# Score products in 32 x 32 pieces, and a new order for the opening of a two-layer transformer kernel

## Chip, cores and metric

The kernel runs on one core of a Trainium2 chip. The metric is the device time of one execution in microseconds (us). TensorE is called PE here, VectorE DVE, ScalarE ACT, GpSimd POOL, and SyncE SP. PE multiplies a stationary operand, which a weight load brings into its array of 128 rows by 128 columns, with a moving operand, and writes PSUM. The other three compute engines do the rest of the arithmetic. SP and ACT issue the transfers of this kernel.

## What is computed

The input x has 2048 rows of 512 numbers in bfloat16. Two layers are applied, each of an attention with 32 heads of 16 dimensions and a feed-forward part with a hidden width of 1792; both layers use the same weights.

```python
def _A_ref(x, wqkv, wo):
    B, S, D = x.shape
    H = 32; Dh = D // H
    qkv = (lambda x, *d: x.transpose(*d))((x @ wqkv).reshape(B, S, 3, H, Dh), 2, 0, 3, 1, 4)
    q, k, v = qkv[0], qkv[1], qkv[2]
    scale = Dh ** -0.5
    scores = jnp.einsum("bhqd,bhkd->bhqk", q, k) * scale
    p = _softmax(scores, axis=-1)
    o = jnp.einsum("bhqk,bhkd->bhqd", p, v)
    return (lambda x, *d: x.transpose(*d))(o, 0, 2, 1, 3).reshape(B, S, D) @ wo

def _B_ref(x, w1, w2):
    h = _silu(jnp.einsum("bsd,df->bsf", x, w1))
    return jnp.einsum("bsf,fd->bsd", h, w2)

x = A_x
x = x + _A_ref(_layernorm(x, axis=-1), A_wqkv, A_wo)
x = x + _B_ref(_layernorm(x, axis=-1), B_w1, B_w2)
x = x + _A_ref(_layernorm(x, axis=-1), A_wqkv, A_wo)
x = x + _B_ref(_layernorm(x, axis=-1), B_w1, B_w2)
```

## The kernel before

**Tiles.** Attention goes by segments: four heads (a head block, hb) by 512 queries (a chunk, c). Within a segment, a score tile is 128 keys by 512 queries for two of the four heads. Each head has 32 rows of the array: 16 for its dimensions and further ones by which a bound on the scores is subtracted. So a score tile is two products (L1214), each with a stationary operand of 32 rows by 128 columns (`KT`, keys) and a moving operand of 32 rows by 512 (`QT`, queries). Each of the two writes one bank of a slot of PSUM. There are three slots. PE may issue one tile or, when two slots are free, two tiles together; four products with different rows then run side by side.

**From scores to output.** Most slots are read by ACT, which writes the exponential in bfloat16 (L1429). About every fifth is read by DVE, which makes an approximation of the exponential by integer arithmetic (L1459), from which POOL (L1520) or DVE (L1493) derives three shifted copies. The value products (L1290) multiply the rows with the values, 17 columns a head (16 dimensions and a column of ones for the sum), in four column strips of the array, one for each head, and add up in `q_ps`.

**Background work.** Projections, the output product, layer norm and the feed-forward part are pieces that are woven between the score tiles. Their products come from the helper `mm` (L282), which while `whole[0]` is false cuts each in four column strips of 128 rows by 32 columns; in the opening and the ending they are whole (L278). Fillers (L1325) keep PE's clock up where nothing else is ready; beside score products they take 32 rows and 16 columns.

**Order.** Each of the four compute engines executes its instructions in the order in which they are written. In the main part a planner (`Flow`) fixes that order when the program is built: it keeps a clock for each engine with fixed costs (`MM`, `SWITCH` and others) and picks, for each engine in turn, the next step. What it picks does not depend on the measured times. The method `scores` writes a tile's products. The planner's order is the same before and after the change, since no cost of it is changed.

**Opening.** Up to the first score tile a list written out by hand, `OPENING`, gives the order: a word such as `s10` is a step and its numbers. s are statistics of a row tile, sq the square root, r the reciprocal, a the normalisation (L201), t a transpose on PE (L215), c its copy by ACT (L1593), k, h and m the keys of the first head block, v and e the values, q, o, u, b, z and y the first queries, w fillers, x a table load. The first digit is the chunk. Ahead of it stand the set-up steps: the loads, constants on POOL, and the weaving of the raw weights `wraw` into `wkq` by POOL (L144), first for five heads, then for the others. These set-up steps are written outside of the manual order, so that their place on each engine is chosen by the framework's own scheduler; the manual order is entered just ahead of `OPENING`.

Of the kernel before, what the change touches and what calls it, by code (L numbers as in the profile page):

```python
# [12 lines left out]
FP32 = mybir.dt.float32  # L13
BF16 = mybir.dt.bfloat16
# [6 lines left out]
def kernel(  # L21
# [22 lines left out]
    NQC = S // 512  # L44
# [3 lines left out]
    EPS = 1e-5  # L48
    KR = 32
    VW = DH + 1  # L50
# [14 lines left out]
    cpool = ctx.enter_context(tc.tile_pool(name="cpool", bufs=1))  # L65
    wpool = ctx.enter_context(tc.tile_pool(name="wpool", bufs=1))
    xpool = ctx.enter_context(tc.tile_pool(name="xpool", bufs=1))
# [17 lines left out]
        return gpool.tile([P, 512], FP32, name=name, tag="g")  # L85


    x_sb = xpool.tile([P, TT, D], BF16, name="x_sb")
    for tt in range(4):
        (nc.scalar if tt % 2 else nc.sync).dma_start(x_sb[:, tt, :], xf[tt * P : (tt + 1) * P, :])  # L90
    for c in range(1, NQC):
        nc.sync.dma_start(
            x_sb[:, 4 * c : 4 * c + 4, :],
            xf[512 * c : 512 * (c + 1), :].rearrange("(tt p) d -> p tt d", p=P),
        )
    wv_sb = wpool.tile([P, CT, D], BF16, name="wv_sb")
    wo_sb = wpool.tile([P, CT, D], BF16, name="wo_sb")
    w1_sb = wpool.tile([P, CT, F], BF16, name="w1_sb")
    w2_sb = wpool.tile([P, FT, D], BF16, name="w2_sb")


    wkq = wpool.tile([P, CT, 2 * D + DH], BF16, name="wkq")
    wraw = htpool.tile([P, CT, 2 * D], BF16, name="wraw", tag="ht")
    nc.scalar.dma_start(wraw[:], A_wqkv[:, 0 : 2 * D].rearrange("(ct p) f -> p ct f", p=P))
    nc.scalar.dma_start(wv_sb[:], A_wqkv[:, 2 * D : 3 * D].rearrange("(ct p) f -> p ct f", p=P))
    nc.sync.dma_start(wo_sb[:], A_wo.rearrange("(ct p) e -> p ct e", p=P))
    nc.sync.dma_start(w1_sb[:], B_w1.rearrange("(ct p) f -> p ct f", p=P))
    nc.sync.dma_start(w2_sb[:], B_w2.rearrange("(ft p) e -> p ft e", p=P))

    ident = cpool.tile([P, P], BF16, name="ident")  # L110
    make_identity(nc, ident[:])
    eps_t = cpool.tile([P, 1], FP32, name="eps_t")
    nc.vector.memset(eps_t[:], EPS)
# [3 lines left out]
    half = cpool.tile([P, 4, 1], FP32, name="half")  # L117
    nc.gpsimd.memset(half[:], -0.5)
# [6 lines left out]
    nc.gpsimd.memset(wkq[:, :, 2 * D : 2 * D + DH], 0.0)  # L125
    E = cpool.tile([P, P], FP32, name="E")
    nc.gpsimd.memset(E[:], 0.0)
    sel = cpool.tile([P, 2, P], BF16, name="sel")
    for j in range(4):
        one = slice(32 * j + 16, 32 * j + 17)  # L130
        nc.gpsimd.tensor_copy(out=E[:, one], in_=ident[:, one])
        nc.gpsimd.memset(E[32 * j : 32 * j + 16, one], -1.0)
        for i in range(2):
# [5 lines left out]
    for lo, hi in ((0, 5), (5, H)):  # L139
        for t in range(2):  # L140
            for ct in range(CT):
                pairs = wkq[:, ct, 0 : 2 * D].rearrange("p (h t d) -> p h t d", t=2, d=DH)
                raw = wraw[:, ct, (1 - t) * D : (2 - t) * D].rearrange("p (h d) -> p h d", d=DH)
                nc.gpsimd.tensor_copy(out=pairs[:, lo:hi, t, :], in_=raw[:, lo:hi, :])  # L144
# [4 lines left out]
    v_flat, x_flat = (xpool.tile([P, TT * H * VW], BF16, name=f"v{i}") for i in range(2))  # L149
    vs = [  # L150
        v[:].rearrange("p (t h w) -> p t h w", t=TT, h=H) for v in (v_flat, x_flat)
    ]
# [82 lines left out]
    def dve(ns, fn, g=""):  # L235
        return ("dve", ns, fn, g)
# [59 lines left out]
    def bank(cell, name):  # L296
        cell["ps"] = narrow(name)
# [36 lines left out]
    def ones_v(L, lo, hi):  # L334
        nc.gpsimd.memset(vs[L][:, lo:hi, :, DH:VW], 1.0)
# [566 lines left out]
    class Flow:  # L902
# [291 lines left out]
        def scores(self, at, picks):  # L1194

            if self.mode != "R":
                at += SWITCH
            self.mode = "R"
            two = len(picks) == 2
            self.pe = at + (MM + 8 if two else MM + 3)  # L1200
            self.runs.append((at, at + MM))
            new = []
            for k in picks:
                t = Tile(self.n)
                self.n += 1
                if t.seg.i > self.started:
                    self.started = t.seg.i
                    self.begin(t.seg)
                if t.pr == 0 and t.kt != t.seg.kts[0]:
                    self.pace(t.seg, t.kt - t.seg.kts[0])  # L1210
                t.slot, t.at = k, at
                for jj in range(2):
                    j = 2 * t.pr + jj
                    nc.tensor.matmul(  # L1214
                        self.slots[k][:, jj, :],
                        lhsT=KT[32 * j : 32 * j + KR, t.seg.hb, t.kt * P : (t.kt + 1) * P],
                        rhs=t.seg.QT[32 * j : 32 * j + KR, :],
                        start=True,
                        stop=True,
                    )  # L1220
# [331 lines left out]
    HOT = 0.9  # L1552
    MOST = 2600

    ordered = {
        mybir.EngineType.PE, mybir.EngineType.Activation, mybir.EngineType.DVE, mybir.EngineType.Pool
    }
# [57 lines left out]
    def o_e(c, i):  # L1615
        tt = 4 * c + 2 * i
        nc.scalar.copy(
            vs[0][:, tt : tt + 2, :, 0:DH],
            at["v", c, i][:].rearrange("p t (h d) -> p t h d", d=DH),
        )  # L1620
        ones_v(0, tt, tt + 2)
        v_made.update([(0, tt), (0, tt + 1)])

    def o_q(_):
# [33 lines left out]
    for word in OPENING.split():  # L1658
        name, args = word.rstrip("0123456789"), [int(d) for d in word if d.isdigit()]
# [49 lines left out]
```

## Time and profile before

| | |
|---|---|
| median of 3 runs | 1651.63 us (1651.11 to 1653.09) |
| the profiled execution | 1650.25 us, span of its trace 1648.5 us |
| PE | 1568.1 us busy, 17480 products |
| ACT | 1592.4 us busy |
| DVE | 1154.7 us busy |
| POOL | 1213.2 us busy |
| first score product | at 37.42 us |

The trace starts with the first instruction of the program. A row of a timeline gives the start, the length from the first to the last of the merged instructions, the engine, the line, what is written and read, and how many instructions. "PEld" are weight loads. In brackets stands the idle time before the row, with what ended it. PE's ends are modelled: a product of 512 columns is recorded with some 380 ns, though the next on the same part of the array starts after about 0.22 us. The chain is the work that ended last, followed back from the end.

### The profile page before, as it was taken

The page shows a single profiled execution, that of the slowest core. Times are in us where ns is not written, and L with a number is a line of the kernel's source. Part 1 is how long each engine was busy: PE and PEld are TensorE (multiplying, and loading weights), DVE is VectorE, ACT ScalarE, POOL GpSimd, SP SyncE. Part 2 cuts the span into 40 slices and gives each one's busy share as a digit, 9 for nine tenths or more (in the row PEclk, how much of TensorE's full clock was granted, in tenths as well). Part 3 has the DMA queues.
Part 4 walks back from the last instruction along what each step waited for, and adds up shares of the span by engine and source line. Part 5 has one row for each costly group of instructions (what it writes and reads, how often), then busy time and mean ns, then how long its engine had stood idle before and what let it go on. Part 6 is the DMA issues. An engine that isn't in the chain of part 4 may idle for free.

```text
span 1648.5 us, 42491 instructions
## 1 busy us (share of the span) xinstructions
PE 1568.1 (95%) x17480; PEld 506.5 (31%) x17480; DVE 1154.7 (70%) x1463; ACT 1592.4 (97%) x1807; POOL 1213.2 (74%) x1290
## 2 busy tenths in 40 slices
PE   7999999999999999999999998999999999999998
PEld 3222223233333333233333232222223323333333
DVE  6778877766777666657776556887666786686744
ACT  5999999999999999999999998999999999999993
POOL 2888988896787767756666654877767897899850
PEclk9999999999999999999999999999999999999999
DMA  5000001010110001000000000011000000010000
GB/s 192 5 8 8 8 5 20 21 8 5 33 21 5 8 21 30 9 8 17 21 15 2 2 14 8 11 11 30 18 8 14 25 21 8 14 34 11 11 24 13
DMA packets 83682, 30.77 MB, mean 19 GB/s; under 512 B 75552, under 2 KB 82464, under 8 KB 83488
## 3 DMA queue, kind: packets, MB, share of 16 engines
q1 hardware_dynamic: 82000, 26.10, 7.2%
q8 instruction: 136, 2.23, 0.6%
q10 hardware_dynamic: 1488, 1.97, 0.3%
q14 instruction: 58, 0.48, 0.1%
HBM read 7.86 MB, written 2.10 MB: 6 GB/s over the span
## 4 chain that ended last, share of the span: by engine, by line
PE 58%; ACT 22%; DVE 8%; issue 6%; POOL 4%; DMA 2%; ACTq 0%; DVEq 0%; POOLq 0%
PE slot L1214 20%; PE q_ps L1290 17%; ACT p L1429 14%; PE y_ps L282 7%; PE q_ps L282 3%; PE h_ps L282 3%; ACT v L1429 3%; PE k_ps L282 3%; ACT t_sb L546 2%; POOL p L1520 2%; DVE p L1459 2%; DVE hT L550 1%; DMA at<-oT 1%; ACT q_old L1429 1%; PE v_ps L282 1%
## 5 line engine op out<-in xcount | busy, mean ns | idle before, releaser
L1429 ACT ACTIVATE p<-slot 128x1024 bf16<-128x1024 f32 x1186 | 1189.8, 1209 | 11.1 <-PE slot L1214 10.3
L1520 POOL TENSOR_TENSOR p<-p,steps 128x512 int32<-128x512 int32 x569 | 595.3, 1069 | 241.9 <-DVE p L1459 201.8
L1290 PE MATMUL q_ps<-p,v 128*17 128x512 bf16 x4590 | 520.9, 382 | 4.3 <-ACT p L1429 1.1
L1214 PE MATMUL slot<-QT,KT 32*128 32x512 bf16 x3104 | 441.9, 381 | 24.3 <-ACT p L1429 10.4
L1459 DVE TENSOR_SCALAR p<-slot 128x1024 uint16<-128x1024 f32 x282 | 344.3, 1221 | 136.1 <-PE slot L1214 121.1
L1214 PEld LDWEIGHTS <-KT 32*128 32x128 bf16 x4096 | 193.3, 91 | 580.5 <-issue 575.3
L1429 ACT ACTIVATE v<-slot 128x1024 bf16<-128x1024 f32 x295 | 338.9, 1234 | 1.7 <-PE slot L1214 1.6
L1290 PEld LDWEIGHTS <-v 128*17 128x17 bf16 x6574 | 165.6, 88 | 286.2 <-issue 225.4
L1290 PE MATMUL q_ps<-v,v 128*17 128x512 bf16 x1302 | 202.8, 381 | 1.9 <-DVE oT L1118 0.9
L1520 POOL TENSOR_TENSOR p<-v,steps 128x512 int32<-128x512 int32 x123 | 129.5, 1066 | 47.6 <-DVE v L1459 34.9
L1520 POOL TENSOR_TENSOR v<-p,steps 128x512 int32<-128x512 int32 x138 | 146.2, 1067 | 23.9 <-DVE p L1459 23.3
L1429 ACT ACTIVATE q_old<-slot 128x1024 bf16<-128x1024 f32 x130 | 154.1, 1222 | 1.0 <-PE slot L1214 1.0
L282 PE MATMUL h_ps<-xnT,w_sb 128*32 128x512 bf16 x1568 | 130.7, 384 | 9.9 <-DVE hT L550 8.9
L1214 PE MATMUL slot<-q_old,KT 32*128 32x512 bf16 x896 | 124.4, 381 | 7.6 <-ACT p L1429 4.9
L1459 DVE TENSOR_SCALAR v<-slot 128x1024 uint16<-128x1024 f32 x82 | 100.1, 1220 | 37.1 <-PE slot L1214 34.9
L550 DVE SCALAR_TENSOR_TENSOR hT<-t_sb,h_ps 128x512 bf16<-128x512 f32 x98 | 66.9, 683 | 79.4 <-ACT t_sb L546 79.4
L282 PE MATMUL y_ps<-w_sb,hT 128*32 128x512 bf16 x1568 | 119.4, 382 | 1.4 <-DVE qc L359 1.1
L1290 PE MATMUL q_ps<-q_old,v 128*17 128x512 bf16 x572 | 98.3, 381 | 1.5 <-DVE q_old L1493 0.7
L282 PE MATMUL q_ps<-xnT,wkq 128*32 128x512 bf16 x1008 | 82.1, 383 | 2.1 <-DVE hT L550 1.2
L282 PE MATMUL k_ps<-xnT,wkq 128*32 128x512 bf16 x960 | 79.3, 383 | 1.8 <-DVE hT L550 0.7
L546 ACT ACTIVATE t_sb<-h_ps 128x512 f32<-128x512 f32 x98 | 76.4, 780 | 0.1
L1520 POOL TENSOR_TENSOR v<-v,steps 128x512 int32<-128x512 int32 x59 | 62.7, 1069 | 10.9 <-DVE v L1459 10.9
(162 smaller groups left out, 1543.6 us busy)
## 6 DMA issues: line engine op xcount, KB each, us to landing
w_sb<-in_B_w_dram SPq DMA_DIRECT2D x2, 1792.0 KB, 15.2
out_dram<-x_sb SPq DMA_DIRECT2D x15, 128.0 KB, 1.7
x_sb<-in_A_x_dram SPq DMA_DIRECT2D x3, 512.0 KB, 10.3
wraw<-in_A_wqkv_dram ACTq DMA_DIRECT2D x1, 1024.0 KB, 8.7
at<-oT SPq DMA_TRANSPOSE x63, 2.3
xnT<-hT SPq DMA_TRANSPOSE x44, 2.3
wv_sb<-in_A_wqkv_dram ACTq DMA_DIRECT2D x1, 512.0 KB, 10.9
wo_sb<-in_A_wo_dram SPq DMA_DIRECT2D x1, 512.0 KB, 11.2
```

Source lines behind the costliest of these rows:

```text
L282: nc.tensor.matmul(ps[g, :], lhsT=lhsT[:, g], rhs=rhs, start=start, stop=stop, skip_group_check=True)
L546: nc.scalar.activation(t_sb, ps, ACT.Tanh, scale=0.5)
L550: nc.vector.scalar_tensor_tensor(out=hT[:, ft, :], in0=t_sb, scalar=1.0, in1=ps, op0=ALU.add, op1=ALU.mult)
L1214: nc.tensor.matmul(self.slots[k][:, jj, :], lhsT=KT[32 * j : 32 * j + KR, t.seg.hb, t.kt * P : (t.kt + 1) * P], rhs=t.seg.QT[32 * j : 32 * ...
L1290: nc.tensor.matmul(self.o_ps[32 * j : 32 * j + VW, :], lhsT=vs[seg.L][:, t.kt, 4 * seg.hb + j, :], rhs=buf[:, jj, :], start=not seg.opened ...
L1429: nc.scalar.activation(buf[:].rearrange("p a b -> p (a b)"), self.slots[x.slot][:].rearrange("p a b -> p (a b)"), ACT.Exp, scale=float(SCALE),
L1459: nc.vector.tensor_scalar(out=whole.bitcast(U16), in0=self.slots[x.slot][:].rearrange("p a b -> p (a b)"), scalar1=float(UNIT), scalar2=fl ...
L1520: nc.gpsimd.tensor_tensor(out=b1.bitcast(I32), in0=b0.bitcast(I32), in1=steps32[:, k : k + 1].to_broadcast([P, 512]), op=ALU.add,)
```

## The change

Three things are changed.

1. Each score product is split in four of 32 columns: product g reads 32 of the 128 keys and writes 32 of the 128 partitions of the same bank. All have the same moving operand.
2. The manual order is entered ahead of the set-up, so that it too runs in written order. The set-up is rewritten: loads of the first five heads' query and key columns come first, ahead of the values' weights, and the other heads' columns follow the input on SP's queue; POOL writes all ones of the first layer's `v` in one step ahead of the first weave, where before each value step wrote its own.
3. `OPENING` is reordered: among other things k0 stands ahead of v00, and sq1 ahead of e00.

```diff
+    ctx.enter_context(tc.manual_schedule(engines=ordered))
...
-    nc.scalar.dma_start(wraw[:], A_wqkv[:, 0 : 2 * D].rearrange("(ct p) f -> p ct f", p=P))
+    FIRST = 5
+    def load_x(c, queue):
+        queue.dma_start(
+            x_sb[:, 4 * c : 4 * c + 4, :],
+            xf[512 * c : 512 * (c + 1), :].rearrange("(tt p) d -> p tt d", p=P),
+        )
+    def load_kq(lo, hi, queue):
+        for t in range(2):
+            at = slice(D * t + DH * lo, D * t + DH * hi)
+            queue.dma_start(wraw[:, :, at], A_wqkv[:, at].rearrange("(ct p) f -> p ct f", p=P))
+    for tt in range(4):
+        (nc.scalar if tt % 2 else nc.sync).dma_start(x_sb[:, tt, :], xf[tt * P : (tt + 1) * P, :])
+    load_kq(0, FIRST, nc.scalar)
+    load_x(1, nc.sync)
     nc.scalar.dma_start(wv_sb[:], A_wqkv[:, 2 * D : 3 * D].rearrange("(ct p) f -> p ct f", p=P))
+    load_x(2, nc.sync)
+    load_x(3, nc.sync)
+    load_kq(FIRST, H, nc.sync)
...
+    def ones_v(L, lo, hi):
+        nc.gpsimd.memset(vs[L][:, lo:hi, :, DH:VW], 1.0)
...
+    def weave(lo, hi):
+        for t in range(2):
+            for ct in range(CT):
+                pairs = wkq[:, ct, 0 : 2 * D].rearrange("p (h t d) -> p h t d", t=2, d=DH)
+                raw = wraw[:, ct, (1 - t) * D : (2 - t) * D].rearrange("p (h d) -> p h d", d=DH)
+                nc.gpsimd.tensor_copy(out=pairs[:, lo:hi, t, :], in_=raw[:, lo:hi, :])
+
     E = cpool.tile([P, P], FP32, name="E")
...
+    ones_v(0, 0, TT)
+    weave(0, FIRST)
+    sel = cpool.tile([P, 2, P], BF16, name="sel")
...
+    weave(FIRST, H)
...
-            ones_v(L, tt, tt + 1)
+            if L:
+                ones_v(L, tt, tt + 1)
...
-                    nc.tensor.matmul(
-                        self.slots[k][:, jj, :],
-                        lhsT=KT[32 * j : 32 * j + KR, t.seg.hb, t.kt * P : (t.kt + 1) * P],
-                        rhs=t.seg.QT[32 * j : 32 * j + KR, :],
-                        start=True,
-                        stop=True,
-                    )
+                    for g in range(0, P, 32):
+                        nc.tensor.matmul(
+                            self.slots[k][g : g + 32, jj, :],
+                            lhsT=KT[32 * j : 32 * j + KR, t.seg.hb, t.kt * P + g : t.kt * P + g + 32],
+                            rhs=t.seg.QT[32 * j : 32 * j + KR, :],
+                            start=True,
+                            stop=True,
+                            skip_group_check=True,
+                        )
...
-    ctx.enter_context(tc.manual_schedule(engines=ordered))
-
     OPENING = """
-        w9 s00 s01 s02 s03 sq0 r0 a00 a01 t00 a02 t01 c00 a03 t02 s10 c01 t03 c02 s11 v00 c03 s12 s13
-        k0 e00 s20 v01 sq1 h0 r1 a10 a11 a12 t10 a13 e01 t11 s21 q0 c10 s22 t12 c11 t13 s23 c12 v10 c13
-        s30 sq2 r2 a20 a21 e10 t20 a22 t21 a23 k1 s31 c20 c21 t22 s32 t23 h1 v20 s33 c22 c23 m0 sq3 k2
-        r3 e20 a30 a31 t30 a32 t31 c30 a33 t32 o0 c31 t33 c32 v21 u0 c33 m1 h2 x0 m2 k3 v11 e21 h3
-        w2 m3 b0 e11 z0 w3 y0
+        w9 s00 s01 s02 s03 sq0 r0 a00 a01 t00 a02 t01 c00 a03 t02 s10 c01 t03 c02 s11 c03 s12 k0 s13 v00
+        h0 sq1 r1 a10 v01 a11 e00 a12 a13 s20 t10 s21 e01 t11 q0 s22 c10 t12 c11 s23 t13 c12 v10 s30 sq2
+        c13 r2 a20 a21 k1 a22 e10 a23 s31 t20 t21 c20 t22 s32 c21 t23 c22 s33 v20 c23 m0 sq3 h1 r3 a30
+        a31 e20 t30 a32 t31 a33 k2 c30 m1 c31 t32 o0 t33 h2 v21 u0 c32 m2 c33 x0 k3 v11 e21 h3 m3 b0 e11
+        w2 z0 w3 y0
     """
...
-        ones_v(0, tt, tt + 2)
```

More of the change, by code (lines that the diff above doesn't have):

```diff
@@ L85, in narrow @@
         return gpool.tile([P, 512], FP32, name=name, tag="g")
+    ordered = {
+        mybir.EngineType.PE, mybir.EngineType.Activation, mybir.EngineType.DVE, mybir.EngineType.Pool
+    }
+    ctx.enter_context(tc.manual_schedule(engines=ordered))
     x_sb = xpool.tile([P, TT, D], BF16, name="x_sb")
[L89 to L94, printed above, removed]
-        )
     wv_sb = wpool.tile([P, CT, D], BF16, name="wv_sb")
@@ L108 @@
     nc.sync.dma_start(w2_sb[:], B_w2.rearrange("(ft p) e -> p ft e", p=P))
+    v_flat, x_flat = (xpool.tile([P, TT * H * VW], BF16, name=f"v{i}") for i in range(2))
+    vs = [
+        v[:].rearrange("p (t h w) -> p t h w", t=TT, h=H) for v in (v_flat, x_flat)
+    ]
+    def ones_v(L, lo, hi):
+        nc.gpsimd.memset(vs[L][:, lo:hi, :, DH:VW], 1.0)
+    eps_t = cpool.tile([P, 1], FP32, name="eps_t")
+    nc.vector.memset(eps_t[:], EPS)
+    nc.gpsimd.memset(wkq[:, :, 2 * D : 2 * D + DH], 0.0)
     ident = cpool.tile([P, P], BF16, name="ident")
     make_identity(nc, ident[:])
-    eps_t = cpool.tile([P, 1], FP32, name="eps_t")
-    nc.vector.memset(eps_t[:], EPS)
+    half = cpool.tile([P, 4, 1], FP32, name="half")
+    nc.gpsimd.memset(half[:], -0.5)
     steps32 = cpool.tile([P, len(SHIFTS)], I32, name="steps32")
@@ L116 @@
         nc.gpsimd.memset(steps32[:, k : k + 1], SHIFTS[k] * 65537)
-    half = cpool.tile([P, 4, 1], FP32, name="half")
-    nc.gpsimd.memset(half[:], -0.5)
     cols = cpool.tile([P, 2], FP32, name="cols")
@@ L124 @@
     own, onescol = (cols[:, i : i + 1] for i in range(2))
-    nc.gpsimd.memset(wkq[:, :, 2 * D : 2 * D + DH], 0.0)
+    def weave(lo, hi):
[4 more added lines that the diff above has]
+                nc.gpsimd.tensor_copy(out=pairs[:, lo:hi, t, :], in_=raw[:, lo:hi, :])
     E = cpool.tile([P, P], FP32, name="E")
     nc.gpsimd.memset(E[:], 0.0)
-    sel = cpool.tile([P, 2, P], BF16, name="sel")
     for j in range(4):
@@ L132 @@
         nc.gpsimd.memset(E[32 * j : 32 * j + 16, one], -1.0)
-        for i in range(2):
+    ones_v(0, 0, TT)
+    weave(0, FIRST)
+    sel = cpool.tile([P, 2, P], BF16, name="sel")
+    for i in range(2):
+        for j in range(4):
             nc.gpsimd.tensor_copy(
@@ L138 @@
     nc.gpsimd.tensor_scalar_mul(out=sel[:, 1, :], in0=sel[:, 1, :], scalar1=-1.0)
[L139 to L144, printed above, removed]
+    weave(FIRST, H)
     KT = xpool.tile([P, HB, S], BF16, name="KT")
@@ L148 @@
     xnTs = [xpool.tile([P, CT, 512], BF16, name=f"xnT{c}") for c in range(NQC)]
[L149 to L152, printed above, removed]
     o_old = [v_flat[:, 1024 * hb : 1024 * (hb + 1)].bitcast(FP32) for hb in range(HB)]
@@ L332 @@
     v_made = set()
-    def ones_v(L, lo, hi):
-        nc.gpsimd.memset(vs[L][:, lo:hi, :, DH:VW], 1.0)
     def v_piece(tt, L):
```

4 lines of the change are left out of this document (removed).

## The prediction

> **What bounds the kernel now.** I read the page first: busy shares, then the chain that ended last, then the costly groups.
>
> ```profile
> span 1648.5 us, 42491 instructions
> ...
> PE 1568.1 (95%) x17480; PEld 506.5 (31%) x17480; DVE 1154.7 (70%) x1463; ACT 1592.4 (97%) x1807; POOL 1213.2 (74%) x1290
> ...
> PE 58%; ACT 22%; DVE 8%; issue 6%; POOL 4%; DMA 2%; ACTq 0%; DVEq 0%; POOLq 0%
> PE slot L1214 20%; PE q_ps L1290 17%; ACT p L1429 14%; PE y_ps L282 7%; PE q_ps L282 3%; PE h_ps L282 3%; ACT v L1429 3%; PE k_ps L282 3%; ACT t_sb L546 2%; POOL p L1520 2%; DVE p L1459 2%; DVE hT L550 1%; DMA at<-oT 1%; ACT q_old L1429 1%; PE v_ps L282 1%
> ...
> L1429 ACT ACTIVATE p<-slot 128x1024 bf16<-128x1024 f32 x1186 | 1189.8, 1209 | 11.1 <-PE slot L1214 10.3
> ...
> L1214 PEld LDWEIGHTS <-KT 32*128 32x128 bf16 x4096 | 193.3, 91 | 580.5 <-issue 575.3
> ...
> L1429 ACT ACTIVATE v<-slot 128x1024 bf16<-128x1024 f32 x295 | 338.9, 1234 | 1.7 <-PE slot L1214 1.6
> L1429 ACT ACTIVATE q_old<-slot 128x1024 bf16<-128x1024 f32 x130 | 154.1, 1222 | 1.0 <-PE slot L1214 1.0
> ```
>
> Two engines are full. ACT takes the exponentials (L1429: 1186 + 295 + 130 of them here) at 97%; PE is at 95%, and the score products alone hold 20% of the chain, 0.20 x 1648.5 = 330 us. The 4096 weight loads of L1214 are two for each score tile, so there are 2048 tiles.
>
> The next view is ACT's timeline. Successive exponentials start 0.90 to 0.91 us apart, though each is recorded as 1.22 to 1.25; the one at 222.99, before which ACT had been idle, took 1.02. So about 0.2 us of a usual record is queueing behind its predecessor.
>
> ```profile
> 209.26 1.22 ACT L1429 ACTIVATE p<-slot 128x1024 bf16<-128x1024 f32 x1
> 210.17 1.24 ACT L1429 ACTIVATE v<-slot 128x1024 bf16<-128x1024 f32 x1
> 211.07 1.25 ACT L1429 ACTIVATE q_old<-slot 128x1024 bf16<-128x1024 f32 x1
> 222.99 1.02 ACT L1429 ACTIVATE v<-slot 128x1024 bf16<-128x1024 f32 x1 [0.59 <-PE slot L1214]
> ```
>
> Hence a score tile that is some 30 ns later usually costs ACT nothing. It costs where ACT's queue has run dry, or where PE itself is the one that is late. The chain by stage shows that both kinds occur: in the first stage below PE's score products hold 33.8% and ACT's L1429 11.0%; in the second 12.6% against 33.4% for p and idle alone.
>
> ```profile
> by line: PE slot L1214 33.8%; PE q_ps L1290 29.5%; PE k_ps L282 16.9%; PE q_ps L282 5.2%; ACT p L1429 4.0%; ACT q_old L1429 3.5%; ACT v L1429 3.5%; DVE p L1459 1.2%; DVE KT L291 0.7%; DVE amax L307 0.7%; issue 0.5%; PE q_ps L1325 0.4%; DVE
> by line: ACT p L1429 24.9%; PE slot L1214 12.6%; PE q_ps L1290 11.5%; issue 8.6%; ACT idle L1429 8.5%; DVE p L1459 6.0%; PE k_ps L282 3.8%; PE q_ps L282 3.3%; DVE idle L1459 2.4%; ACT f_sb L465 2.4%; DMA at<-oT 2.3%; DVE QT L442 2.0%; DVE o
> ```
>
> (The stages are 100 to 200 us and 1000 to 1100 us.)
>
> **The split score products.** PE's timeline gives the prices.
>
> ```profile
> 599.97 0.12 PEld L282 LDWEIGHTS <-wkq 128*32 128x32 bf16 x8 [0.23 <-issue]
> 599.97 0.62 PE L282 MATMUL q_ps<-xnT,wkq 128*32 128x512 bf16 x8
> 600.57 0.39 PE L1214 MATMUL slot<-QT,KT 32*128 32x512 bf16 x2
> 600.89 0.61 PE L282 MATMUL q_ps<-xnT,wkq 128*32 128x512 bf16 x8
> ...
> 1103.11 0.39 PE L1214 MATMUL slot<-QT,KT 32*128 32x512 bf16 x2
> 1103.43 0.38 PE L1325 MATMUL q_ps<-wo_sb,wkq 32*16 32x512 bf16 x1
> 1103.74 0.39 PE L1290 MATMUL q_ps<-p,v 128*17 128x512 bf16 x2
> L282 PEld LDWEIGHTS <-wkq x1968: 92/93/98, 51.2 to 1570.3; 128*32 128x32 bf16 x197
> ```
>
> The background products are already cut in four column strips, and the first row shows what that costs: eight weight loads of 93 ns each fit in 0.12 us, so they start (120 - 93) / 7 = 4 ns apart. Four strips run side by side: eight products, two rounds of four, take 0.62 = 0.39 + a round of about 0.22. So a strip on its own part of the array costs its issue, some 4 ns, and no streaming time.
>
> A tile has 2 products before and 8 after: 6 x 4 = 24 ns more until its last one has started; a group of two tiles (x4 in the trace, 16 after) 48 ns more. Over all tiles that is 2048 x 24 ns = 49 us of PE time, the outer bound if every one of them counted. On the chain:
>
> ```profile
> 300.83 0.33 PE slot L1214 x4
> 301.16 0.53 PE q_ps L1290 x6
> 301.70 0.31 PE q_ps L282 x4
> 302.01 0.32 PE slot L1214 x2
> ```
>
> A score group holds 0.32 to 0.33 us of the chain here, others a little more; with 0.36 the chain's 330 us are some 900 groups, about half of them singles, half pairs: 900 x 36 ns = 32 us. That is the cost if the chain stayed as it is. But the chain's ACT pieces, 22% = 363 us or 300 exponentials of 1.21, carry (1.21 - 1.02) = 0.19 us of queueing each, 57 us in all, more than the 32. Where the stage is ACT's, the delay vanishes in that queue; where it is PE's (100 to 200 us: 34 us of score products on the chain) it does not. I count two to three such stages of 34 us out of 330, or a quarter: 32 x 0.25 = **8 us**. Bounds: 0 (all absorbed) and 32.
>
> Row to row the order of tiles stays, and no product gets a new wait: the first of a tile waits for the slot, the last releases the exponential. Behind a late tile on PE stand value products (L1290) and background products (L282); ACT, DVE's exponentials (L1459) and through them Pool's shifts wait for it.
>
> **Changing the array's shape.** Between score and background products PE starts 0.32 us after the last product (600.57 to 600.89), not 0.22: some 0.1 us goes at each change of shape. Could 32 x 32 strips spare it? The filler product at 1103.43 has just that shape. It starts 0.32 after a 32 x 128 product and is followed after 0.31 by a 128-row one. So 32 by 32 next to 128 rows still pays, and I take nothing for it. The Trainium skill says so too (TensorEngine Tiling (Array Packing), Key Properties): changing the tiling mode, not just the tile, drains the engine. By that rule the change spares no drain, and the trace agrees with its 0.31.
>
> **The opening.** Here work moves, on four engines and two queues.
>
> ```profile
> 2.14 10.90 DMA wv_sb<-in_A_wqkv_dram
> ...
> 8.66 2.05 ACT L1593 COPY xnT<-t_ps 128x512 bf16<-128x512 bf16 x4 [1.40 <-PE t_ps L215]
> 10.39 0.44 POOL L144 COPY wkq<-wraw 128x80 bf16<-128x80 bf16 x2 [8.78 <-DMA wraw<-in_A_wqkv_dram]
> 13.09 3.23 PE L278 MATMUL v_ps<-wv_sb,xnT 128*128 128x512 bf16 x8 [3.41 <-DMA wv_sb<-in_A_wqkv_dram]
> 13.36 0.18 DVE L175 BATCH_NORM_AGGREGATE mvb<-st 128x2 f32<-128x6 f32 x1
> 16.15 1.03 PE L278 MATMUL k_ps<-xnT,wkq 128*128 128x512 bf16 x4
> 16.35 1.01 ACT L1617 CAST v<-v_ps 128x1024 bf16<-128x1024 f32 x1 [5.64 <-PE v_ps L278]
> 17.26 0.30 ACT L1576 ACTIVATE std<-mvb,eps_t 128x4 f32<-128x4 f32 x1
> 17.46 0.77 ACT L1603 ACTIVATE KT<-k_ps,cols 128x512 bf16<-128x512 f32 x1
> 17.59 0.18 DVE L1582 RECIPROCAL rstd<-std 128x4 f32<-128x4 f32 x1 [4.05 <-ACT std L1576]
> 17.81 3.66 DVE L201 TENSOR_SCALAR v<-x_sb,mvb,rstd 128x512 bf16<-128x512 bf16 x4
> 18.74 0.90 PE L215 MATMUL t_ps<-ident,v 128*128 128x128 bf16 x8
> 37.42 0.40 PE L1214 MATMUL slot<-QT,KT 32*128 32x512 bf16 x4
> ```
>
> PE and ACT stand from 10.7 to 13.1 for wv; then ACT's copy of the values (16.35) keeps the second chunk's square root waiting, so DVE's reciprocal comes at 17.59 although the statistics were done at 13.54. After the change the first heads' weights are 80 columns a side instead of the whole 1 MB, and k0 stands ahead of v00. It can start when the last copy of the first chunk is done, 8.66 + 2.05 = 10.7, and runs 4 x 0.40 (the rate of the eight at 13.09) to 12.4; h0 (0.77) and the square root (0.30) follow, the reciprocal comes at about 13.9: 3.7 us earlier. PE keeps less: k0 (1.7), v00 (3.2) and v01 (8 x 0.22 = 1.8 at the later rate) end at 17.4, and the transposes that started at 18.74 gain 1.3. Between 1.3 and 3.7 I take **2.5 us** for the first score product at 37.42, and nothing downstream eats it, since each stage after that starts from there. Bounds: a loss of 1, if the narrow rows of the first weights land late or Pool reaches them late (its list now has E's columns and all the ones of v ahead of those copies), and a gain of 4. ACT's queue has one issue more ahead of wv; SP's has two more ahead of wo, w1 and w2, which have no user in the opening. Pool's later weave has until the second head block, after 40 us.
>
> **The sum.** The profiled execution took 1650.25 (span 1648.5 and 1.75 around it), 1.4 under the median 1651.63. 1651.63 + 8 - 2.5 = **1657**. Own range: 1651.63 + 0 - 4 = 1648 to 1651.63 + 32 + 1 = 1685.
>
> **Rivals.**
>
> *PE's feed becomes the bound (slower still).* After the change PE has 17480 + 12288 = 29768 products and as many loads. Over 1650 us that is one pair each 55 ns; before it was one each 94.
>
> ```profile
> 721.80:753.80 32.00, 32.00 (x447) 11.52 (x447) 15.09 (x19) 32.00 (x36) 16.78 (x23) 1.00 0.03 6
> ```
>
> The densest 32 us I found had 447 pairs, 72 ns each: nothing here shows a steady 55. Against the rival: products start 4 ns apart once queued, and PE's waits before are for other engines. It decides where a pair needs more than 55 ns; at 60 the time is 29768 x 0.060 = 1786. Chance 0.08. The Trainium skill (TensorE: Matmul & The Clock Gate, "Wait — 56ns, not 53.3ns?") says that with hardware decode off the sequencer spends about 62 ns on each matmul, which bounds where the array's work is shorter. By it, an estimate would be 29768 x 0.062 = 1846; no run here shows which way this PE decodes.
>
> *The slack takes it all (faster).* If ACT's queue absorbs every late tile, also in the PE stages, the score term is 0 and the opening alone is left: 1651.63 - 2.5 to - 4 = 1648 to 1649. For it: ACT waits for PE's slots only 10.3 + 1.6 + 1.0 us in all. Against it: the stage at 100 to 200 us. It decides where PE catches up before each dry queue. Chance 0.27, half of it beyond 0.2% when the opening gives its 4 or more.
>
> *The drain goes (much faster).* If 32 x 32 strips change to 128 rows without the 0.1 us, 900 groups save two each, 180 us, more than ACT leaves: the 1611 exponentials of the rows above need 1611 x 0.905 = 1458 of the 1611 us after 37.42, and the other 153 hold ACT's other work and the ending. With a third of these, 51, as the gain: 1651.63 - 51 - 2.5 = 1598. It decides where a change of shape costs under about 0.07. Against it stands 1103.74. Chance 0.05.
>
> *PE stages everywhere.* The whole 32 counts: 1651.63 + 32 - 2.5 = 1681. Chance 0.15.
>
> **How the numbers follow.** The forecast's case has 0.45, with the other four 0.08, 0.27, 0.05 and 0.15. About 0.2%, 3.3 us, is what a measurement of this kernel tells from no change. Faster by more: 0.05 + 0.14 + 0.06 of the forecast's low end = 0.25. Within: 0.13 of the slack case + 0.07 = 0.20. Slower: 0.55. The range leaves out the drain, the feed and the edges: 1644 to 1690.
>
> **What would show it.** Right: 16384 products on the score line, their starts about 4 ns apart; 0.31 to 0.32 us still at each change of shape; the first score product near 35 us; exponentials still 0.90 apart in ACT's stages; score products with a larger share of the chain. Wrong: starts of strips spread over more than 100 ns in a pair (the feed), changes of shape at 0.22 (the drain), or the first score product at 37 or later (the opening).

## The result and the profile after

The changed kernel took 1648.66 us (median of 20 runs, 1643.73 to 1651.99), the kernel before 1651.95 us beside it (20 runs). The ratio is 0.9977, with a 95% interval of 0.9968 to 0.9987: a gain of 0.23%, or 3.8 us, where a loss, to 1657 us, was forecast. The profiled execution took 1649.16 us, with a span of 1647.3.

These are the lines of the page of after that answer to those shown of before: busy times, the chain by engine and by line, and the groups of exponentials and score loads.

```profile
PE 1576.1 (96%) x29768; PEld 523.4 (32%) x29768; DVE 1153.2 (70%) x1463; ACT 1593.8 (97%) x1807; POOL 1212.7 (74%) x1281
...
PE 62%; ACT 22%; DVE 8%; issue 5%; POOL 2%; DMA 1%; ACTq 0%; DVEq 0%; POOLq 0%
PE slot L1237 22%; PE q_ps L1314 18%; ACT p L1453 14%; PE y_ps L306 7%; PE h_ps L306 4%; PE q_ps L306 3%; ACT v L1453 3%; PE k_ps L306 3%; ACT t_sb L568 2%; DVE p L1483 2%; DVE hT L572 1%; POOL p L1544 1%; ACT q_old L1453 1%; PE v_ps L306 1%; PE q_ps L1349 1%
...
L1453 ACT ACTIVATE p<-slot 128x1024 bf16<-128x1024 f32 x1186 | 1168.6, 1150 | 12.9 <-PE slot L1237 11.3
...
L1237 PEld LDWEIGHTS <-KT 32*32 32x32 bf16 x16384 | 209.9, 88 | 574.4 <-issue 567.6
```

The 16384 pieces are there, and the share of score products in the chain rose from 20% to 22%, as announced. The exponentials tell something else: the mean record of the 1186 that write `p` fell from 1209 to 1150 ns. ACT did not become faster. Each record contains the wait behind the exponential before it, and that wait became 59 ns shorter, because the tiles come later.

The tile view of the slots gives the time from the first to the last score product of these operands. First before, then after:

```profile
L1214 PE MATMUL slot<-QT,KT x3104: 371/384/386, 37.4 to 1603.3; 32*128 32x512 bf16 x194
```

```profile
L1237 PE MATMUL slot<-QT,KT x12416: 370/385/605, 32.7 to 1602.1; 32*32 32x512 bf16 x198
```

The first of these products came 4.7 us earlier, the last 1.2. So in these two executions the opening gave 4.7 us and the main part took 3.5 back. The experiments part the two.

### The profile page after: what moved, and what is told of

Read it like the earlier page. It is cut to its first block, busy times and chain, and to the rows that moved or that the text cites. A ratio compares the mean times of both kernels' runs of the same rounds, so it can differ in the third digit from the quotient of the medians.

```text
span 1647.3 us, 67061 instructions
## 1 busy us (share of the span) xinstructions
PE 1576.1 (96%) x29768; PEld 523.4 (32%) x29768; DVE 1153.2 (70%) x1463; ACT 1593.8 (97%) x1807; POOL 1212.7 (74%) x1281
## 4 chain that ended last, share of the span: by engine, by line
PE 62%; ACT 22%; DVE 8%; issue 5%; POOL 2%; DMA 1%; ACTq 0%; DVEq 0%; POOLq 0%
PE slot L1237 22%; PE q_ps L1314 18%; ACT p L1453 14%; PE y_ps L306 7%; PE h_ps L306 4%; PE q_ps L306 3%; ACT v L1453 3%; PE k_ps L306 3%; ACT t_sb L568 2%; DVE p L1483 2%; DVE hT L572 1%; POOL p L1544 1%; ACT q_old L1453 1%; PE v_ps L306 1%; PE q_ps L1349 1%
## 5 line engine op out<-in xcount | busy, mean ns | idle before, releaser
L1453 ACT ACTIVATE p<-slot 128x1024 bf16<-128x1024 f32 x1186 | 1168.6, 1150 | 12.9 <-PE slot L1237 11.3
L1237 PE MATMUL slot<-QT,KT 32*32 32x512 bf16 x12416 | 462.5, 384 | 22.7 <-ACT p L1453 9.6
L1237 PEld LDWEIGHTS <-KT 32*32 32x32 bf16 x16384 | 209.9, 88 | 574.4 <-issue 567.6
L1453 ACT ACTIVATE v<-slot 128x1024 bf16<-128x1024 f32 x295 | 323.4, 1164 | 2.3 <-PE slot L1237 2.0
L1453 ACT ACTIVATE q_old<-slot 128x1024 bf16<-128x1024 f32 x130 | 146.2, 1152 | 0.1
L1237 PE MATMUL slot<-q_old,KT 32*32 32x512 bf16 x3584 | 130.4, 384 | 6.8 <-ACT p L1453 3.8
L568 ACT ACTIVATE t_sb<-h_ps 128x512 f32<-128x512 f32 x98 | 70.8, 723 | 0.0
L1349 PE MATMUL q_ps<-wo_sb,wkq 128*16 128x512 bf16 (+1 forms) x203 | 70.1, 380 | 0.0
```

The lines of the kernel that those rows point to most:

```text
L568: nc.scalar.activation(t_sb, ps, ACT.Tanh, scale=0.5)
L1237: nc.tensor.matmul(self.slots[k][g : g + 32, jj, :], lhsT=KT[32 * j : 32 * j + KR, t.seg.hb, t.kt * P + g : t.kt * P + g + 32], rhs=t.seg. ...
L1349: nc.tensor.matmul(out[0:DH, :], lhsT=wkq[rows, 0, 2 * D : 2 * D + DH], rhs=wo_sb[rows, 0, :], start=out is not self.o_ps, stop=out is not ...
L1453: nc.scalar.activation(buf[:].rearrange("p a b -> p (a b)"), self.slots[x.slot][:].rearrange("p a b -> p (a b)"), ACT.Exp, scale=float(SCALE),
```

## The experiments

All ratios are to the kernel before on the same chip. The theories were: A, that ACT's queue takes up the later tiles until it runs dry, so that the price of the split is convex in the delay; B, that score products on the chain pay for every nanosecond, so that the price is proportional to it. For the opening, the loads, the written order of the set-up and the new list were rivals. The last two columns are of one execution each: with the opening of before, the first score product came at 37.42 us and in e2 at 39.02, where PE's wait for `wv` ended 1.2 us later.

| kernel | median us | ratio, 95% | first score product, us | mean record of p, ns |
|---|---|---|---|---|
| after | 1648.66 | 0.9977 (0.9968 to 0.9987) | 32.74 | 1150 |
| e1: opening alone | 1644.84 | 0.9952 (0.9939 to 0.9965) | 31.29 | 1203 |
| e2: split alone | 1655.25 | 1.0013 (1.0003 to 1.0022) | 39.02 | 1151 |
| split64 | 1646.63 | 0.9968 (0.9956 to 0.9981) | 31.39 | 1168 |
| delay128 | 1654.46 | 1.0015 (1.0002 to 1.0028) | 32.95 | 1089 |
| delay256 | 1689.78 | 1.0223 (1.0205 to 1.0241) | 31.26 | 1038 |
| halves | 1656.07 | 1.0021 (1.0009 to 1.0033) | 31.25 | 1111 |
| loads only | 1647.09 | 0.9976 (0.9965 to 0.9987) | 32.52 | 1203 |
| set-up only | 1649.56 | 0.9991 (0.9981 to 1.0000) | 36.93 | 1207 |
| new list only | 1652.32 | 1.0003 (0.9993 to 1.0014) | 37.49 | 1196 |
| old list, new loads and set-up | 1646.41 | 0.9962 (0.9949 to 0.9975) | 30.60 | 1199 |

### The two halves of the change

e1 is the changed kernel with the two whole score products of before:

```diff
-                    for g in range(0, P, 32):
-                        nc.tensor.matmul(self.slots[k][g : g + 32, jj, :], ... + g + 32 ...)
+                    nc.tensor.matmul(self.slots[k][:, jj, :], lhsT=KT[... : (t.kt + 1) * P], ...)
```

> The whole change but for the score products, which stay two of 128 columns a tile. Theory A (the split costs little since ACT's queue of exponentials takes the delay; the opening gains what its first score product shows): 4 to 5 us faster than before, ratio 0.997, so about 1 to 1.5 us faster than the changed kernel; the first score product at 32.7 us, mean record of an exponential back at 1.21 us. Theory B (the chain's PE stages charge the split in full, a quarter to all of it, and something in the order of the opening hides it): 8 us or more faster than the changed kernel, ratio to before 0.993 or lower. Theory C (the split itself is a gain and the opening is not kept): no faster than before.

e2 is the kernel before with the new loop over `g` alone.

> Before with the split score products alone, old set-up and opening. Theory A: 1 to 4 us slower than before (ratio 1.001 to 1.002), first score product at 37.4 us, mean record of an exponential about 1.15 us. Theory B: 8 to 32 us slower. Theory C: 2 to 4 us faster.

The opening alone gains 0.48%, 7.9 us against the median of before beside it (1653.32); the split alone costs 0.13%, 2.1 us. Their product, 0.9952 x 1.0013 = 0.9965, agrees with 0.9977 within the intervals. e1 is faster than both given kernels. By after against e1, 0.9977 against 0.9952, the split costs 0.25% or 4 us. So its price is 2 to 4 us, not 8. The granted clock of PE, which differs between executions, shifts these medians: it was 0.994 in the median of the runs of before beside them, 0.995 in e2's and 0.996 in e1's. Among runs with the same clock, e2 took 3.5 us more than before at 0.995 (1656.1 against 1652.6 on the mean) and 3.1 at 0.996, and e1 took 5.4 and 6.1 less. So the split costs 3 to 4 us rather than 2, and the opening gains 5 to 6 rather than 7.9; 4 to 5 had been expected of e1.

### How much later a tile is

split64 cuts each product in two strips of 64 columns instead of four of 32.

```diff
-                    for g in range(0, P, 32):
+                    for g in range(0, P, 64):
...
-                            self.slots[k][g : g + 32, jj, :],
-                            lhsT=KT[... : t.kt * P + g + 32],
+                            self.slots[k][g : g + 64, jj, :],
+                            lhsT=KT[... : t.kt * P + g + 64],
```

> The changed kernel with score products split in two of 64 columns instead of four of 32. If the latency of a tile grows with its count of products (theory A): four products a tile, last start 11 ns after the first, mean record of an exponential between 1.209 (two) and 1.150 us (eight), about 1.19; time between the opening alone and the change, 0 to 2 us faster than the changed kernel. If it is the narrow strip itself that is slow: 1.15 to 1.17 and the time of the changed kernel.

The cleanest place to read the delay is the first pair of tiles, for which ACT has been waiting. The timelines of before, split64 and after, in this order (start, length, and in brackets ACT's idle time):

```profile
37.42 0.40 PE L1214 MATMUL slot<-QT,KT 32*128 32x512 bf16 x4
37.84 1.94 ACT L1429 ACTIVATE p<-slot 128x1024 bf16<-128x1024 f32 x2 [1.04 <-PE slot L1214]
```

```profile
31.39 0.42 PE L1237 MATMUL slot<-QT,KT 32*64 32x512 bf16 x8
31.85 1.94 ACT L1453 ACTIVATE p<-slot 128x1024 bf16<-128x1024 f32 x2 [1.07 <-PE slot L1237]
```

```profile
32.74 0.44 PE L1237 MATMUL slot<-QT,KT 32*32 32x512 bf16 x16
33.21 1.94 ACT L1453 ACTIVATE p<-slot 128x1024 bf16<-128x1024 f32 x2 [1.09 <-PE slot L1237]
```

From the first product to ACT it is 0.42, 0.46 and 0.47 us. The row of a pair grows from 0.40 to 0.44, 40 ns for 12 more products, 3 to 4 ns each as forecast. Over all tiles, the median spread from a tile's first to its last product is 5 ns before, 10 in split64 and 23 after. But in these first pairs the time from the start of the first tile's last product to ACT is also longer: 423 ns before, 445 in split64, 452 after. These 20 to 30 ns the forecast did not have, and the runs do not show where they come from. A tile is thus about 50 ns late, twice the 24 ns counted; ACT's mean record lost 59 ns. split64 does not part the two explanations: its mean record of 1168 ns is what was expected if the narrow strip itself were slow, its time, 2 us below that of after, what was expected if the count of products decides.

### What a further delay costs

delay128 and delay256 add to the changed kernel one filler product ahead of each tile, of 32 rows by 16 columns with 128 or 256 columns of moving data. It writes to the slot and is overwritten by the tile. It takes time on PE too, so these runs do not part a delay from more work on PE.

```diff
+                r0 = slice(64 * t.pr, 64 * t.pr + KR)
+                nc.tensor.matmul(
+                    self.slots[k][0:DH, 0, 0:128], lhsT=wkq[r0, 0, 2 * D : 2 * D + DH], rhs=wo_sb[r0, 0, 0:128],
+                    start=True, stop=True, skip_group_check=True,
+                )
                 for jj in range(2):
```

> The changed kernel with one filler of 32 rows, 16 columns and 128 columns of moving operand ahead of each score tile, on the same rows, written to the tile's slot, where the tile's products then overwrite it; each tile is late by some 53 to 57 ns more. Theory A: the queue in front of ACT had 1150 - 1018 = 132 ns left on the mean, so most of the delay is taken again: mean record of an exponential about 1.10 us, the kernel 3 to 12 us slower than the changed one. Theory B (chain): 900 groups x 55 ns, at a quarter to all of it 12 to 50 us slower.

> The same with a filler of 256 columns: each tile late by some 107 to 112 ns more. Theory A: the queue runs dry for a large part of the tiles, so the cost per ns grows: mean record about 1.06 us, 25 to 60 us slower than the changed kernel, well over twice what 128 columns cost. Theory B (chain): in proportion, twice of what 128 columns cost, 24 to 100 us slower.

The delays are estimates: 53 ns for 128 columns at the rate of 0.22 us for 512, and 107 for 256; ACT's mean record lost 61 and 112 ns. The first cost 1654.46 - 1648.66 = 6 us, the second 41. The fillers also went with a higher granted clock (0.999 in the median of delay128, 0.997 in after); at equal clocks, 0.998 and 0.999, delay128 cost 9 to 11 us over after and delay256 43. So twice the delay costs four to seven times as much, and the first one less than the 12 us that B had at the least. The group rows of the exponentials, first delay128, then delay256, show the queue being used up:

```profile
L1458 ACT ACTIVATE p<-slot 128x1024 bf16<-128x1024 f32 x1186 | 1148.1, 1089 | 16.4 <-PE slot L1242 13.5 <-PE q_ps L1319 0.6 <-POOL p L1549 0.4
```

```profile
L1458 ACT ACTIVATE p<-slot 128x1024 bf16<-128x1024 f32 x1186 | 1145.1, 1038 | 18.6 <-PE slot L1242 11.6 <-PE q_ps L1319 0.9 <-ACT v L1458 0.5
```

An exponential that waits for nothing is recorded with 1018 ns. So the mean wait in ACT's queue is 1209 - 1018 = 191 ns before, 132 after, 71 with delay128 and 20 with delay256. The first 50 to 60 ns cost 2 to 4 us, the next 6 (9 to 11 at equal clocks), the last 35. PE had slack as well: the view of waits (us in total, times, longest) gives PE waiting for an exponential to free a slot, before, after and with delay256, where L1235 is the filler ahead of the tile:

```profile
PE slot L1214 <- ACT p L1429: 16.1, 66, 0.5
```

```profile
PE slot L1237 <- ACT p L1453: 14.1, 58, 0.5
```

```profile
PE slot L1235 <- ACT p L1458: 3.6, 14, 0.4
```

### Whether the feed of PE is near

halves cuts each 32 by 32 product of after in two of 256 queries, 16 a tile and 46152 pairs of load and product in all.

```diff
-                for jj in range(2):
+                for h, jj in ((h, jj) for h in range(0, 512, 256) for jj in range(2)):
...
-                            self.slots[k][g : g + 32, jj, :],
+                            self.slots[k][g : g + 32, jj, h : h + 256],
...
-                            rhs=t.seg.QT[32 * j : 32 * j + KR, :],
+                            rhs=t.seg.QT[32 * j : 32 * j + KR, h : h + 256],
```

> The changed kernel with every strip split again in two of 256 queries, 16 products a tile: 46152 products and loads, one pair each 36 ns over the run. If PE's feed is a bound (rival of the prediction, deciding at 55 ns a pair): 29768 pairs already run, so the limit is under 46 ns; a limit of 40 would make it 46152 x 0.040 = 1846 us. Theory A (the feed is no bound, only latency counts): a tile's last product starts some 110 ns later, but streams 107 ns less, so its result is 0 to 40 ns later than in the changed kernel: 0 to 8 us slower than that.

It cost 0.21% + 0.23%, some 7 us over after, within the 0 to 8 expected if the feed is no bound, and PE kept up. The densest 32 us that I found, in after and in halves (columns: PE, PEld, DVE, ACT and POOL busy with counts, granted clock, DMA share, GB/s):

```profile
1408.10:1440.10 32.00, 32.00 (x702) 10.24 (x698) 21.60 (x25) 32.00 (x36) 27.30 (x26) 1.00 0.05 15
```

```profile
1420.70:1452.70 32.00, 32.00 (x1068) 11.18 (x1068) 23.15 (x25) 32.00 (x36) 27.13 (x27) 1.00 0.09 21
```

That is 46 ns a pair in after and 30 in halves, with the same 36 instructions of ACT in 32.00 busy us. The feed is no bound of this change.

### What in the opening gains

old_list is e1 with the `OPENING` of before; it keeps the new loads and the written-order set-up.

> Whole score products, the new set-up and loads, but the old list of the opening (v00 ahead of k0, sq1 behind e00). Theory A (the loads carry the gain: the values' weights no longer wait behind 1 MB): v00 starts about 10.5 us instead of 13.1, the first score product near 34 to 35, 2.5 to 4 us faster than before. Theory B (the list carries it): the first score product at 36 or later, within 1.5 us of before.

new_list_only is the kernel before with the new `OPENING` alone.

> Whole score products, the old set-up and loads, the new list. Theory A (loads): k0 now stands ahead of v00 and still waits for the whole raw weights, woven at about 13.7, so the first score product is at 36 or later, no faster than before by more than 1.5 us. Theory B (list): first score product at 34 or earlier, 3 to 5 us faster. If the two parts only work together, both this run and the one with the old list gain less than half of the 4.7 to 6.1 us.

loads_only is the kernel before with the new loads alone (`load_x` and `load_kq` as in the change):

```diff
-    for c in range(1, NQC):
-        nc.sync.dma_start(x_sb[:, 4 * c : 4 * c + 4, :], ...)
...
-    nc.scalar.dma_start(wraw[:], A_wqkv[:, 0 : 2 * D].rearrange("(ct p) f -> p ct f", p=P))
+    load_kq(0, FIRST, nc.scalar)
+    load_x(1, nc.sync)
     nc.scalar.dma_start(wv_sb[:], A_wqkv[:, 2 * D : 3 * D].rearrange("(ct p) f -> p ct f", p=P))
+    load_x(2, nc.sync)
+    load_x(3, nc.sync)
+    load_kq(FIRST, H, nc.sync)
```

> Before with the new order of the loads alone: whole score products, the set-up outside of the manual order, the old list. Theory A (the loads carry the opening's gain, since the values' weights land earlier): v00 starts at 9.5 to 10.5 us, the first score product at 32 or earlier, 4 to 8 us faster than before. Theory B (the loads help only with the set-up in written order, where Pool weaves the first heads as soon as they land): Pool's weave or the list's k0 is late, first score product at 34 or later, at most 3 us faster.

setup_only is old_list with the loads of before, so that the written-order set-up is left alone.

> Whole score products, the set-up in written order, but the old loads (the whole raw weights, then the values' weights) and the old list. Theory A: v00 still waits until about 13, the first score product is at 36.5 to 38, the time within 1.5 us of before. Theory B (the written order carries it): 3 us faster or more.

The loads give 0.24%, the set-up 0.09% at the edge of its interval, both together 0.38%, the new list nothing: alone 1.0003, and on top of the two 0.9952 against 0.9962, which overlap. The loads alone thus gave some 4 us, at the low end of what was expected of them, and the first score product came at 32.52, not by 32. The timelines say why the loads gain and the list does not. First the weaving and the keys in new_list_only, then values and keys in loads_only:

```profile
9.63 0.44 POOL L144 COPY wkq<-wraw 128x80 bf16<-128x80 bf16 x2 [8.02 <-DMA wraw<-in_A_wqkv_dram]
...
13.78 1.89 PE L278 MATMUL k_ps<-xnT,wkq 128*128 128x512 bf16 x4 [4.40 <-POOL wkq L144]
```

```profile
9.80 1.90 PE L290 MATMUL v_ps<-wv_sb,xnT 128*128 128x512 bf16 x8 [0.32 <-DMA wv_sb<-in_A_wqkv_dram]
...
12.45 1.04 PE L290 MATMUL k_ps<-xnT,wkq 128*128 128x512 bf16 x4 [0.74 <-POOL wkq L156]
```

With k0 first but the old loads, PE stands 4.40 us for POOL's weaving, whose first copies start at 9.63, when the 1 MB of raw weights is there, and whose later ones stand between other work of POOL. With the new loads the values stand first, as before, and start at 9.80 instead of 13.09, because wv is no longer queued behind that megabyte. The page's list of transfers has it (size, and median us from issue to landing), after first, then before:

```profile
x_sb<-in_A_x_dram SPq DMA_DIRECT2D x3, 512.0 KB, 7.1
...
wv_sb<-in_A_wqkv_dram ACTq DMA_DIRECT2D x1, 512.0 KB, 7.2
```

```profile
x_sb<-in_A_x_dram SPq DMA_DIRECT2D x3, 512.0 KB, 10.3
...
wv_sb<-in_A_wqkv_dram ACTq DMA_DIRECT2D x1, 512.0 KB, 10.9
```

In loads_only wv took 7.0 us.

What the set-up in written order adds to the loads shows in DVE's normalisation of the second chunk. First loads_only, with POOL beside it, then old_list:

```profile
13.19 3.38 DVE L213 TENSOR_SCALAR v<-x_sb,mvb,rstd 128x512 bf16<-128x512 bf16 x4
12.91 1.88 POOL L347 MEMSET v<- 128x64 bf16 x7
14.39 4.54 POOL L156 COPY wkq<-wraw 128x432 bf16<-128x432 bf16 x8
```

```profile
12.97 1.38 DVE L225 TENSOR_SCALAR v<-x_sb,mvb,rstd 128x512 bf16<-128x512 bf16 x4
14.53 4.02 POOL L155 COPY wkq<-wraw 128x432 bf16<-128x432 bf16 x8 [3.10 <-DMA wraw<-in_A_wqkv_dram]
```

The four normalisations took 3.38 us and 1.38, and the first score product came at 32.52 and 30.60. It is the same in the other runs of this set: 3.4 to 4.1 us where the framework placed the set-up (before, e2, new_list_only) and POOL was writing the ones and weaving meanwhile, 1.38 in after, e1 and setup_only, where POOL stood almost all of that time. That POOL's work holds DVE up is a reading of these rows; no run changed it alone, and the first chunk's normalisations took some 0.41 us each beside POOL's copies too.

## Why the prediction was wrong

**The sign.** The forecast was +8 - 2.5; measured are about +2 to +4 and -8 by the medians, or 5 to 6 of the 8 at equal clocks (+3.5 and -4.7 in the profiled execution of after). The rival nearest to it is the one in which the slack takes it all and the opening decides. Its time, 1648 to 1649, was met partly by luck: the split did cost something, and the opening gave more than the rival's 2.5 to 4. Both terms were mis-sized, and both errors made the forecast too slow.

**The split: 8 us counted, 2 to 4 measured.** The step that failed is the quarter of the chain counted in full. I took 100 to 200 us for a stage of PE, since its score products held 33.8% of the chain there. Two views of the same stretch say otherwise. The windows, before and then after:

```profile
100.00:200.00 100.00, 99.47 (x1116) 30.09 (x1117) 79.76 (x98) 100.00 (x111) 88.17 (x87) 1.00 0.03 7
```

```profile
100.00:200.00 100.00, 97.95 (x1931) 30.09 (x1927) 81.17 (x98) 99.92 (x110) 86.96 (x86) 1.00 0.04 8
```

ACT was busy for all of these 100 us, and PE for 99.47: the chain goes to PE where its last releaser was PE, and does not show that ACT had no work queued. Take the time from the first score product to the pair for which PE waits on `QT`. The four rows are of before, e2, e1 and after:

```profile
222.50 0.40 PE L1214 MATMUL slot<-QT,KT 32*128 32x512 bf16 x4 [0.79 <-DVE QT L383]
```

```profile
224.13 0.44 PE L1215 MATMUL slot<-QT,KT 32*32 32x512 bf16 x16 [0.79 <-DVE QT L383]
```

```profile
216.46 0.40 PE L1236 MATMUL slot<-QT,KT 32*128 32x512 bf16 x4 [0.79 <-DVE QT L405]
```

```profile
218.33 0.44 PE L1237 MATMUL slot<-QT,KT 32*32 32x512 bf16 x16 [0.79 <-DVE QT L405]
```

It is 222.50 - 37.42 = 185.08 before and 224.13 - 39.02 = 185.11 in e2; 216.46 - 31.29 = 185.17 in e1 and 218.33 - 32.74 = 185.59 after. The split costs 0.03 to 0.4 us in the stretch for which the forecast's quarter implied some 3.4 (a tenth of 34). That the delay per tile was twice as long as counted, 50 ns instead of 24, changed little, since the queue still held 132 ns of it. The price falls later and a little at a time: by the 401st score tile after had lost 0.8 us to old_list, whose score products are whole, by the 601st 1.3 and by the 1201st 2.2. Which waits it is there, the runs do not part.

**The opening: 2.5 us counted, 4.7 to 8 measured.** The reciprocal came earlier as forecast (13.9 said). But that does not need k0 ahead of v00: in old_list, with v00 first, it came at 12.76, in e1 at 12.55. This is after's timeline:

```profile
10.33 1.87 PE L302 MATMUL k_ps<-xnT,wkq 128*128 128x512 bf16 x4 [1.08 <-ACT xnT L1612]
11.99 4.42 PE L302 MATMUL v_ps<-wv_sb,xnT 128*128 128x512 bf16 x16
13.23 0.18 DVE L1601 RECIPROCAL rstd<-std 128x4 f32<-128x4 f32 x1 [1.33 <-ACT std L1595]
13.44 1.38 DVE L225 TENSOR_SCALAR v<-x_sb,mvb,rstd 128x512 bf16<-128x512 bf16 x4
16.25 0.61 PE L239 MATMUL t_ps<-ident,v 128*128 128x128 bf16 x8
```

The failing step is that PE gives most of it back. I let the transposes gain 1.3; they came 18.74 - 16.25 = 2.5 us earlier in after, and 3.9 in e1:

```profile
10.49 1.02 PE L302 MATMUL k_ps<-xnT,wkq 128*128 128x512 bf16 x4 [1.09 <-ACT xnT L1610]
11.35 3.62 PE L302 MATMUL v_ps<-wv_sb,xnT 128*128 128x512 bf16 x16
14.81 0.61 PE L239 MATMUL t_ps<-ident,v 128*128 128x128 bf16 x8
```

For k0, v00 and v01 I counted 1.7 + 3.2 + 1.8 = 6.7 us. They took 14.81 - 10.49 = 4.3 in e1 and 5.9 in after. The first two of these terms came from the row at 13.09 of before, whose eight products started 0.38 us apart, not 0.22, because PE's granted clock stood at half there (0.50 in the windows from 13 to 15 us). I took a slowed row for the rate; the last section has the clock.

And the next stretch gained again, where I had let nothing change: from the transposes to the first score product it was 37.42 - 18.74 = 18.68 us, now 32.74 - 16.25 = 16.49. The windows of before and after show the engine that was full there:

```profile
18.00:32.00 14.00, 11.46 (x85) 5.92 (x83) 13.65 (x32) 10.46 (x19) 3.00 (x10) 1.00 0.43 155
```

```profile
18.00:32.00 14.00, 13.46 (x84) 6.57 (x84) 10.96 (x29) 12.43 (x21) 0.66 (x2) 1.00 0.46 165
```

DVE was busy for 13.65 of the 14 us in before, and the chain of before goes over DVE from the reciprocal at 17.59 to 25.2 us. Its four normalisations took 3.66 us there and take 1.38 now, which is the size of this second gain, 2.2 us. In after DVE is busy for 10.96, and the chain goes over PE and ACT from k0 on, with PE at 13.46. The named cause was wrong too: I put the gain down to k0 ahead of v00, but the list is worth nothing by itself. It is wv and the first heads' weights that arrive sooner, and the set-up in written order; I had costed the smaller first load only as something that makes k0 possible, and had not asked what stood behind the megabyte in ACT's queue.

**What held.** Strips start 3 to 4 ns apart. From the start of a tile's last 32 by 32 piece to a product of 128 rows it is still 314 to 315 ns, and 309 the other way (312 before), so no drain is saved; without a change of shape it is some 217. By the rule of the Trainium skill (TensorEngine Tiling (Array Packing), Key Properties) a change of mode drains the engine, and the trace, with its 314, agrees. Exponentials stay 0.90 us apart. The estimate of 1846 from the 62 ns a product of the Trainium skill (TensorE: Matmul & The Clock Gate, "Wait — 56ns, not 53.3ns?") does not hold here: the measured 30 ns a pair excludes it. The time lay within the range, at its fast end, and by luck: the opening gave more than its own bound of 4 us, and the 2 to 4 us of the split made up for it.

## What to carry to other kernels

Ask of a delay on a shared path how much queueing stands in the records of the engine that it feeds (the mean record less the shortest), and compare the two: here the first 50 to 60 ns of a queue of 191 cost 2 to 4 us, the last 50 cost 35. A share of the chain tells who released last, not who has no slack; read the busy time of both engines in that window before counting a share as a price. When a load is made smaller, list what is queued behind it: here that was most of the gain, and the reordering of the work none. Before a row of a trace is taken as a rate, look at the clock that was granted there.

## What was not expected of the hardware

PE's granted clock falls to half for about 3.4 us, or a multiple of it, at a time, at places that differ between kernels and executions. These are the windows of 10 to 18 us in before, after and e1; the last two have the same list and loads:

```profile
10.00:18.00 8.00, 4.91 (x17) 2.00 (x18) 3.73 (x12) 2.36 (x5) 7.24 (x32) 0.79 1.07 404
```

```profile
10.00:18.00 8.00, 7.62 (x36) 3.42 (x36) 6.39 (x20) 3.80 (x7) 4.77 (x15) 0.79 1.07 393
```

```profile
10.00:18.00 8.00, 7.34 (x45) 3.78 (x45) 6.99 (x21) 5.41 (x10) 4.86 (x16) 1.00 1.07 393
```

At 0.79 the four products of k0 took 1.87 us and not 1.02, and the first score product came at 32.74 and not 31.29; most of what the tables show between these two openings is this.

The Trainium skill (TensorE: Matmul & The Clock Gate, Part 1) has half the rate after an idle window of about 3.4 us that runs freely, so that the effect varies from run to run. That fits the four kernels with the old loads (before, e2, set-up only, new list only): PE stood 3.4 to 5.0 us for `wv` or for POOL's weaving, and its products then started at half clock; this window has 0.79, 0.57, 0.64 and 0.57. So a part of what the loads gain is a stretch at half clock that e1, old_list and loads_only do not have. It does not fit the opening of after, where PE had idled only some 1.1 us, nor the main part. In after PE was busy for 2.0 to 3.0 of the 3.4 us ahead of each of its three stretches there, and throughout the one at 1201 us:

```profile
1200.00:1205.00 5.00, 5.00 (x83) 1.16 (x79) 1.82 (x3) 4.28 (x5) 3.03 (x3) 0.66 0.01 3
```

What one such stretch costs shows in e1 against old_list, whose score products are the same. They keep in step within 0.03 us for the first 600 score tiles; behind e1's stretch at 609 us e1 is 1.1 us late. From the 1400th score tile (1108 us in e1) to the 1600th (1265), which holds this place and another at 1126 us, after fell 3.1 us behind e1, which had none there. Up to the 1400th it had lost nothing against e1, but e1 had had three by then (609, 981 and 1056 us) and after one behind the opening (983). Against old_list, from the first score tile to the 1201st, in which neither has one, after took 915.17 us against 913.02: these 2.2 us are the split's own. So the 3.5 us above are the split's in part and the clock's in part. The differences of several us between executions of one kernel go with the clock too: of the 20 runs of after, the four with a mean granted clock of 0.995 took 1651.2 us on the mean, the four with 0.999 took 1645.3.

The runs do not show that the split makes such stretches more frequent: the median granted clock was 0.995 in e2 and 0.994 in before beside it. What sets them off in the main part, and why a tile's result is 20 to 30 ns later when its product is cut in strips, stays open.
